# Moving a projection unit forward, eleven scores between the last projection units, and a first attention round cut in two

## The chip, the cores and the metric

The kernel runs on one core of a Trainium2 chip. The metric is the device time of one execution in microseconds (us). The engines of the core are TensorE (PE; its weight loads are shown as PEld), VectorE (DVE), ScalarE (ACT), GpSimd (POOL) and SyncE (SP). Each works through its own queue in the order in which the kernel issues its instructions, and waits for the others by semaphores.

## The reference, cut to what matters

Sequence S = 2048, model width D = 448, 16 heads of width 28, hidden width F = 1792, all float32. The output mixes an attention block and a gated MLP, by a gate for each token:

```python
g = sigmoid((x * gate_w).sum(-1, keepdims=True))
q, k, v = split_heads(x @ wqkv)                 # 16 heads, 28 wide
a = softmax(q @ k.T * 28 ** -0.5) @ v @ wo      # per head, then joined
gate, up = x @ W_gate, x @ W_up
b = (gate * (gate > 0) * up) @ W_down
out = g * a + (1 - g) * b
```

## The kernel before

The projection works in float32r with each operand split into a high and a low part, so one tile of a projection takes 11 matmuls (`TERMS`). Stages, in order:

**Loading.** SyncE loads x in four blocks of 512 tokens (`load_x`, L219) and the projection weights in six slices (`load_w`, L186; `w0` to `w5`, two staging buffers "wr"). ScalarE makes the high parts (`act_high`, L85), VectorE the low parts (`low`, L91); `split_x` and `split_w` issue both.

**Projection units.** There are 44 units. `qk(tb, c)` (L250) makes 128 of the 896 Q and K columns for token block tb: 11 matmuls (L253), a high part by ScalarE and a low part by VectorE into a staging tile `st` (three buffers), and a store by GpSimd to `qk_d` in HBM (L257). `vproj(tb, t)` (L259) makes V for 128 tokens: 11 matmuls (L262) and two ScalarE reads (L265, L266). A unit's PSUM tile comes from `ps_any` (L246), which goes round four banks: two of the scores' ("s"), "x" and "po". Seven `qk` units are written out by hand (L295 to L312); qk(3,0) is the one that first uses the last token block. The others stand in the list `mixed`, where `qk` and `vproj` alternate. At fixed places in it stand `split_w(w5)`, `split_w(w3)`, the loads of head 1's K and Q, and the spills of x.

**Row maxima.** `smax(k)` (L139) makes 128 x 1024 scores of a head (L147, two matmuls into a tile with two buffers) and VectorE reduces them to their maximum (L149). From unit `first` on, `smax` calls are spread evenly behind the units, 2 x `LEAD` = 48 of them. `smax_end` (L154) puts a head's maxima as two extra rows into Q, in float32r halves.

**Scores.** `scores(i, j)` (L168) makes one 128 x 512 tile of the transposed scores of key tile i, with the maxima taken off by the extra rows (L173, PSUM tag "s", two buffers), and ScalarE takes exp of it into `PT[i]` (L175). Four of them (j = 0 to 3) make one key tile. `pv(i)` (L408) then multiplies with V into one accumulator (L413, PSUM tag "po").

**Rounds.** The attention runs in rounds. A round's string says the order on TensorE: "s" a score, "m" a maximum, "x" a matmul of the gate and up projections (`gu_mm`, L380). The scores run one key tile ahead of `pv`. Behind a round's string come the splits of the next gate and up weights (`split_f`, L364; high by ScalarE, low by GpSimd), and then its `pv`. Before the first round four scores, (0,0) to (0,3), have been made: one behind each of the last three units and one after them. The first round is SHORT without its "x": 16 scores and 8 maxima, then four `pv`. The second is SHORT with 11 "x". `small_things` runs at round starts; in the round that starts at key tile 4 it issues `gates` (L348: one ScalarE and three VectorE operations).

**The rest.** The remaining gate and up work, the output projection, the down projection and the mix follow the attention, and are not touched.

Of the kernel before, what the change touches and what calls it, by code (L numbers as in the profile page):

```python
# [27 lines left out]
NB = 4  # L28
# [4 lines left out]
NQ = 2 * D // P  # L33
WARM = 13


LEAD = 24

SHORT = "smsxxsmsxsmsxmsxsmsxxsmsxsmsxxsmsxs"

LONG = "ssmmxsxxsxsmxxsxsmsxxsxxsmmsxxsxxsxsmsxxsmsmsxsxxsxmsmsxxxxsmxssxxmsxsmsxxsmsxmss"
WIDE = "msxxsmsxsxmsxxsxmsxxxxmssmxsxxsxxsmxmssxxxxsxsmsmsxxxxsxsmsxmsxxsxxxsmsmxxxsxsxxxsxmssxmxxss"

LATE = "sxsxxsxsxxsxsxxsxsxxsxsxxsxsxxsxsxsxsx"

ROUNDS = [(SHORT, 0), (SHORT, 1)] + [(LONG, 3)] * 9 + ([(WIDE, 4)] + [(LONG, 3)] * 8) * 2 + [(WIDE, 4)] + [(LATE, 2)] * 6
NP = 9


# [10 lines left out]
def gated_mix_kernel(ctx, tc, x, wq, wo, wgu, wd, out):  # L60
# [8 lines left out]
    def f32(ap):  # L69
        return ap.bitcast(F32)  # L70

    def ps_s(name):
        return psum.tile([P, TB], F32, tag="s", bufs=2, name=name)
# [4 lines left out]
    def ps_o(name):  # L78
        return psum.tile([P, TB], F32, tag="po", bufs=1, name=name)
# [4 lines left out]
    def act_high(dst, src):  # L84
        nc.scalar.activation(dst, src, AF.Copy)  # L85
# [4 lines left out]
    def low(dst, src, high):  # L90
        nc.vector.tensor_tensor(dst, src, f32(high), op=OP.subtract)  # L91
# [22 lines left out]
    def p_slot(k, name, dt=F32):  # L114
        if k in (5, 6):
            return V[:, k - 3].rearrange("p k h d -> p (k h d)").rearrange("p (j t) -> p j t", t=TB)
        return (vp if k < 5 else att).tile([P, 4, TB], dt, name=name, tag=f"P{k}", bufs=1)
# [9 lines left out]
    def load_k(h):  # L127
        for r in range(4):
            nc.sync.dma_start(f32(K[h % 3])[DH * r:DH * (r + 1)], qk_d[r % 2, 2 * DH * h:2 * DH * h + DH, :])

    def load_q(h):
        Q[h] = q_slot(f"Q_{h}").rearrange("p j t -> p (j t)")
        for r in range(4):
            nc.sync.dma_start(f32(Q[h])[DH * r:DH * (r + 1)], qk_d[r // 2, 2 * DH * h + DH:2 * DH * (h + 1), :])
# [4 lines left out]
    def smax(k):  # L139

        h, u, half = maxima[k]
        if u == 0 and half == 0:
            MX[h] = keep.tile([P, 32], F32, name=f"mx_{h}", tag="mx", bufs=2)
        ps = ps_w(f"sm_{k}")
        for c in range(2):
            k0 = (half * 2 + c) * TB
            nc.tensor.matmul(ps[:, c, :], Q[h][:GD, u * P:(u + 1) * P], K[h % 3][:GD, k0:k0 + TB],  # L147
                             start=True, stop=True)
        nc.vector.tensor_reduce(MX[h][:, 2 * u + half:2 * u + half + 1], ps, axis=AX.XY, op=OP.max)  # L149
        if u == NK - 1 and half == 1:  # L150
            M[h] = keep.tile([P, 16], F32, name=f"m_{h}", tag="m", bufs=2)
            nc.vector.tensor_reduce(M[h], MX.pop(h).rearrange("p (a b) -> p a b", b=2), axis=AX.X, op=OP.max)
# [15 lines left out]
    def scores(i, j):  # L168
        h, kt = divmod(i, NK)
        if j == 0:  # L170
            PT[i] = p_slot(i % NP, f"P_{i}")
        ps = ps_s(f"s_{i}_{j}")
        nc.tensor.matmul(ps, K[h % 3][:GD + 2, kt * P:(kt + 1) * P], Q[h][:GD + 2, j * TB:(j + 1) * TB],  # L173
                         start=True, stop=True)
        nc.scalar.activation(PT[i][:, j], ps, AF.Exp, scale=SCALE)  # L175
# [3 lines left out]
    def xf(tb, b):  # L179
        return X[tb][b // 4][:, b % 4]  # L180


    with tc.tile_pool(name="qkv", bufs=1) as pa:
        W = pa.tile([P, 7, 2 * D + VC], F32R, name="W")

        def load_w(c):  # L186
            c0, c1 = c * 2 * GD, (c + 1) * 2 * GD if c < G + 1 else 2 * D + VC
            wr = pa.tile([P, 4, 2 * GD + 2], F32, name=f"wr_{c0}", tag="wr", bufs=2)[:, :, :c1 - c0]
            nc.sync.dma_start(wr, wq[:, :, c0:c1])
            return wr, c0, c1  # L190

        def split_w(wr, c0, c1):

            ways = [(W[:, :, c0:c1], wr)]
            if c0 < 2 * D:
                w, r = (ap.rearrange(f"p c {n} -> p c a j d", a=2, j=4)
                        for ap, n in ((W[:, :, c0:c1], "(j a d)"), (wr, "(a j d)")))
                ways = [(w[:, :, a], r[:, :, a]) for a in range(2)]
            for w, r in ways:
                act_high(w[:, 0:3], r[:, 0:3])  # L200
                low(w[:, 3:6], r[:, 0:3], w[:, 0:3])
            for w, r in ways:
                act_high(w[:, 6], r[:, 3])
                low(w[64:, 6], r[64:, 3], w[64:, 6])
# [36 lines left out]
        def spill_x(tb, r):  # L241
            nc.gpsimd.dma_start(x_d[tb, r], f32(X[tb][r]))

        turn = [3]

        def ps_any(name):  # L246
            turn[0] += 1
            return (ps_s, ps_s, ps_x, ps_o)[turn[0] % 4](name)

        def qk(tb, c, terms=TERMS):  # L250
            ps = ps_any(f"qk_{tb}_{c}")
            for n, (a, b) in enumerate(terms):
                nc.tensor.matmul(ps, W[:, a, c * P:(c + 1) * P], xf(tb, b), start=(n == 0), stop=(n == NT - 1))  # L253
            st = pa.tile([P, 2, TB], F32R, name=f"st_{tb}_{c}", tag="st", bufs=3)
            act_high(st[:, 0], ps)
            low(st[:, 1], ps, st[:, 0])
            nc.gpsimd.dma_start(qk_d[:, c * P:(c + 1) * P, tb * TB:(tb + 1) * TB].rearrange("r d t -> d r t"), f32(st))  # L257
# [21 lines left out]
        ps = ps_o("warm_ps")  # L279
# [29 lines left out]
        w4 = load_w(4)  # L309
        qk(2, 0)  # L310
        w5 = load_w(5)
        qk(3, 0)  # L312
        split_w(*w4)
        w3 = load_w(3)
        load_k(0)
        load_q(0)

        units = [(qk, 2, 1), (qk, 1, 2), (qk, 3, 1), (qk, 2, 2), (qk, 3, 2)]
        units += [(qk, tb, c) for c in range(3, NQ) for tb in range(NB - 1, -1, -1)]
        vs = [(vproj, tb, t) for tb in range(NB - 1, -1, -1) for t in range(4)]  # L320
        mixed = units[:3]
        units = units[3:]
        while units or vs:
            mixed += units[:1] + vs[:1]
            units, vs = units[1:], vs[1:]
        m, first = 0, 8
        spills = {16 + 3 * k: (NB - 1 - k // 2, k % 2) for k in range(6)}
        for n, (f, *a) in enumerate(mixed):
            if n == 1:
                split_w(*w5)  # L330
            if n == 3:
                split_w(*w3)
            if n == 6:
                load_k(1)
                load_q(1)
            if n in spills:
                spill_x(*spills[n])
            f(*a)
            if n >= len(mixed) - 3:
                scores(0, n + 3 - len(mixed))  # L340
            while m < 2 * LEAD and n >= first and m < (n + 1 - first) * 2 * LEAD / (len(mixed) - first):
                smax(m)
                m += 1
                if m == 2 * NK + 3:
                    smax_end(0)
        assert m == 2 * LEAD, m

    def gates():  # L348
        e = const.tile([P, NK], F32, name="e")
# [55 lines left out]
    NI = H * NK  # L405
# [53 lines left out]

    done = sum(n for _, n in ROUNDS) // 2  # L460
    nxt = parts = i0 = 0
# [22 lines left out]
    fetch_f(1)  # L484
    load_k(2)
    load_q(2)
    scores(0, NB - 1)
    wor = None
    for r, (order, nu) in enumerate(ROUNDS):
        ni = order.count("s") // NB  # L490
        late = "m" not in order
        todo = list(range(nxt, nxt + nu))
        nxt += nu
        small_things(i0 // 4)
        if m % (2 * NK) == 0 and i0 <= NI - LEAD:
            smax_end(m // (2 * NK) - 1)
        if late and wor is None:
            wor = load_wo()
        ns = nx = 0
        for o in order:  # L500
            if o == "s":
                i, j = i0 + 1 + ns // NB, ns % NB
                if ns == 4 * NB:
                    small_things(i0 // 4 + 1)
                if i < NI:
                    scores(i, j)
                ns += 1
            elif o == "m":
                smax(m)
                m += 1  # L510
            elif nx < NT * nu:
                i, half = divmod(todo[nx // NT], 2)
                if nx % NT == 0:
                    ps = ps_w(f"gu_{i}_{half}")[:, 0] if late else ps_x(f"gu_{i}_{half}")
                gu_mm(ps, i, half, nx % NT)
                nx += 1
                if nx % NT == 0:
                    (spill_h if half else relu)(i, ps)

        ready = nxt + (ROUNDS[r + 1][1] if r + 1 < len(ROUNDS) else 2)  # L520
        ready += ready % 2
        while parts < ready:
            split_f(parts // 2, pool_low, (parts % 2,))
            parts += 1
            if parts % 2 == 0:
                fetch_f(parts // 2 + 1)
        for i in range(i0, i0 + ni):
            pv(i)
            if i == NI - NK // 2:
                split_wo(wor)  # L530
        i0 += ni
# [154 lines left out]
```

## Time and profile before

| | |
|---|---|
| median of three runs | 1312.54 us (1311.17 to 1313.77) |
| the profiled execution | 1315.21 us, its span 1313.4 us |
| TensorE busy | 1300.0 us (99%) |
| VectorE, ScalarE, GpSimd busy | 799.4 (61%), 770.5 (59%), 360.8 us (27%) |
| granted TensorE clock | 0.999 |
| HBM traffic | 148.87 MB, 113 GB/s over the span |

Busy times are unions of the profile's records, and matmuls overlap each other in them: a busy TensorE may still issue its matmuls with pauses. Pauses are read from the starts of neighbouring matmuls and from the idle times that the timeline prints in square brackets, with what ended them. The span is what lies between the first and the last instruction; the execution's time holds 1.8 us more.

### The profile page before, as it was taken

The numbers are of one execution on the slowest core, as the hardware profiler recorded it, in microseconds if no ns is written. First come the engines' busy times: TensorE is split into PE (matmuls) and PEld (weight loads), VectorE is DVE, ScalarE is ACT, GpSimd is POOL, SyncE is SP. The second block draws the span as 40 slices with busy tenths as digits, with TensorE's granted clock in tenths as the row PEclk, the third lists the DMA queues.
The fourth block names the chain that finished last, engine by engine and source line by source line (L and its number), as shares of the span: only waits on it lengthen the run. The fifth ranks groups of instructions, "written<-read, shape, count | busy, mean of one in ns | idle before, by whom it ended". The sixth has DMA issues, their size and how long they took to land.

```text
span 1313.4 us, 17652 instructions
## 1 busy us (share of the span) xinstructions
PE 1300.0 (99%) x6689; PEld 907.0 (69%) x6689; DVE 799.4 (61%) x811; ACT 770.5 (59%) x1454; POOL 360.8 (27%) x496
## 2 busy tenths in 40 slices
PE   9999999999999999999999999999999999999998
PEld 5888666666666666666666666666666556789997
DVE  6577776676767666766767676767666003663332
ACT  5212686667676676766767667676766785222121
POOL 3212113222222232332313222222322235451020
PEclk9999999999999999999999999999999999999999
DMA  8845515142343624142525324151431225534432
GB/s 294 287 166 219 168 58 106 58 110 67 87 86 91 171 63 89 57 97 66 136 68 158 81 72 97 48 105 41 113 108 55 100 64 180 190 114 147 141 103 74
DMA packets 53533, 148.87 MB, mean 113 GB/s; under 512 B 9992, under 2 KB 17096, under 8 KB 48840
## 3 DMA queue, kind: packets, MB, share of 16 engines
q1 hardware_dynamic: 36520, 98.80, 29.2%
q0 software_dynamic: 16928, 48.93, 10.4%
q8 instruction: 53, 0.87, 0.3%
q14 instruction: 32, 0.26, 0.1%
HBM read 102.06 MB, written 46.02 MB: 113 GB/s over the span
## 4 chain that ended last, share of the span: by engine, by line
PE 93%; DMA 3%; issue 1%; DVE 1%; POOL 1%; ACT 1%; SPq 0%; POOLq 0%; ACTq 0%; DVEq 0%
PE gu L383 21%; PE s L173 19%; PE sm L147 18%; PE po L413 17%; PE acc L606 10%; PE qk L253 3%; PE wo L558 3%; PE v L262 2%; DMA K<-qk_d 1%; DMA qk_d<-st 1%; POOL on L94 1%; DMA wr<-wq 0%; DMA xr<-x 0%; DMA wdr<-wd 0%; PE mt L157 0%
## 5 line engine op out<-in xcount | busy, mean ns | idle before, releaser
L149 DVE TENSOR_REDUCE mx<-sm 128x1 f32<-128x1024 f32 x512 | 610.9, 1220 | 189.5 <-PE sm L147 188.3
L175 ACT ACTIVATE P<-s 128x512 f32<-128x512 f32 x800 | 455.0, 597 | 111.1 <-PE s L173 76.1
L173 PE MATMUL s<-Q,K 114*128 114x512 f32 x1024 | 400.7, 405 | 0.4 <-ACT P L175 0.3
L383 PE MATMUL gu<-X,wg 128*128 128x512 f32 x1232 | 397.0, 396 | 0.0
L147 PE MATMUL sm<-K,Q 112*128 112x512 f32 x1024 | 312.2, 396 | 0.7 <-DMA K<-qk_d 0.5
L173 PEld LDWEIGHTS s<-Q,K 114*128 114x128 f32 x1024 | 190.6, 188 | 108.9 <-ACT P L175 53.1
L383 PEld LDWEIGHTS gu<-X,wg 128*128 128x128 f32 x1232 | 233.5, 190 | 43.9 <-issue 0.8
L147 PEld LDWEIGHTS sm<-K,Q 112*128 112x128 f32 x1024 | 193.0, 190 | 46.6 <-DVE mx L149 2.7
L413 PE MATMUL po<-P,V 128*32 128x512 f32 x1600 | 181.9, 594 | 0.0
L94 POOL TENSOR_TENSOR wg<-wgr,wg 128x384 fp32r<-128x384 f32 x153 | 142.2, 941 | 99.8 <-issue 48.7
L175 ACT ACTIVATE V<-s 128x512 f32<-128x512 f32 x224 | 128.2, 598 | 33.2 <-PE s L173 21.2
L402 POOL DMA_DIRECT2D h_d<-h x56 | 31.7, 566 | 412.2 <-DVE h L396 382.0
L606 PE MATMUL acc<-WD,hh 128*128 128x448 f32 x672 | 140.9, 368 | 0.0
L606 PEld LDWEIGHTS acc<-WD,hh 128*128 128x128 f32 x672 | 126.1, 188 | 12.8
L413 PEld LDWEIGHTS po<-P,V 128*32 128x32 f32 x1600 | 49.1, 110 | 110.5 <-issue 110.5
L85 ACT ACTIVATE hh<-hr 128x512 fp32r<-128x512 f32 x56 | 35.2, 631 | 122.4 <-PE acc L606 118.6
L91 DVE TENSOR_TENSOR hh<-hr,hh 128x512 fp32r<-128x512 f32 x56 | 53.7, 960 | 64.4 <-ACT hh L85 64.4
L396 DVE TENSOR_TENSOR h<-gu,rl 128x512 f32<-128x512 f32 x56 | 38.6, 689 | 87.5 <-PE gu L383 37.3
L253 PE MATMUL qk<-X,W 128*128 128x512 f32 x308 | 76.6, 397 | 2.0 <-ACT X L85 1.8
L253 PEld LDWEIGHTS qk<-X,W 128*128 128x128 f32 x308 | 57.3, 188 | 18.4 <-ACT X L85 2.9
L85 ACT ACTIVATE wg<-wgr 128x384 fp32r<-128x384 f32 x168 | 68.0, 489 | 0.0
L413 PE MATMUL po<-V 128*32 128x512 f32 x448 | 54.1, 594 | 0.0
(58 smaller groups left out, 573.6 us busy)
## 6 DMA issues: line engine op xcount, KB each, us to landing
wgr<-wgu SPq DMA_DIRECT2D x56, 512.0 KB
qk_d<-st POOLq DMA_DIRECT2D x28, 512.0 KB, 3.5
K<-qk_d SPq DMA_DIRECT2D x64, 224.0 KB
Q<-qk_d SPq DMA_DIRECT2D x64, 224.0 KB
h_d<-h POOLq DMA_DIRECT2D x56, 256.0 KB, 2.3
hr<-h_d SPq DMA_DIRECT2D x56, 256.0 KB
x_d<-X POOLq DMA_DIRECT2D x6, 1024.0 KB, 5.0
X<-x_d SPq DMA_DIRECT2D x24, 256.0 KB
```

Source lines behind the costliest of these rows:

```text
L85: nc.scalar.activation(dst, src, AF.Copy)
L91: nc.vector.tensor_tensor(dst, src, f32(high), op=OP.subtract)
L94: nc.gpsimd.tensor_tensor(dst, src, f32(high), op=OP.subtract)
L147: nc.tensor.matmul(ps[:, c, :], Q[h][:GD, u * P:(u + 1) * P], K[h % 3][:GD, k0:k0 + TB], start=True, stop=True)
L149: nc.vector.tensor_reduce(MX[h][:, 2 * u + half:2 * u + half + 1], ps, axis=AX.XY, op=OP.max)
L173: nc.tensor.matmul(ps, K[h % 3][:GD + 2, kt * P:(kt + 1) * P], Q[h][:GD + 2, j * TB:(j + 1) * TB], start=True, stop=True)
L175: nc.scalar.activation(PT[i][:, j], ps, AF.Exp, scale=SCALE)
L253: nc.tensor.matmul(ps, W[:, a, c * P:(c + 1) * P], xf(tb, b), start=(n == 0), stop=(n == NT - 1))
L383: nc.tensor.matmul(ps, WS[i][:, s, a], xf(i // NF, b), start=(n == 0), stop=(n == NT - 1))
L413: nc.tensor.matmul(PO[h][32 * j:32 * j + 32], V[:, h // 4 % 2, kt, h % 4], PT[i][:, j], start=(kt == 0), stop=(kt == NK - 1))
L558: nc.tensor.matmul(ps[:, t % 2, :D], ON[tb][b // 4][:, b % 4, t * P:(t + 1) * P], WO[:, a], start=(n == 0), stop=(n == NT - 1))
L606: nc.tensor.matmul(ACC[tb][t][:, :D], hh[:, a, t * P:(t + 1) * P], WD[:, f, b], start=(f == 0 and n == 0), stop=(f == NF - 1 and n == 2))
```

## The change

Five edits, all of them before the third round:

- qk(2,1) moves from the head of `mixed` to a place ahead of qk(3,0). `mixed` then has 36 units and not 37.
- 50 maxima and not 48 stand behind the units, from the unit with number 9 in `mixed` on, and not 8. Behind the units counted from the end (`EARLY`) stand 2, 3, 3 and 3 scores, eleven in all, ahead of the maxima of the same unit. The single scores behind the last three units and the one after them are gone.
- The four units of the last 128 columns (c = 6) take their PSUM tile from "x" and "po" alone.
- The first round becomes two of two key tiles each. The first has 2 maxima and the one score (2,3) that is left of its eight; the second has 8 scores and 4 maxima.
- The rounds skip the scores that are already made. The number of scores, maxima and all other matmuls is as before. `split_f(0)` stands behind the second of the two rounds.

```diff
+EARLY = (4, 4, 3, 3, 3, 2, 2, 2, 1, 1, 1)
...
-ROUNDS = [(SHORT, 0), (SHORT, 1)] + [(LONG, 3)] * 9 + ([(WIDE, 4)] + [(LONG, 3)] * 8) * 2 + [(WIDE, 4)] + [(LATE, 2)] * 6
+ROUNDS = [("sssssssmms", 0), ("smssmssmsmss", 0), (SHORT, 1)] + [(LONG, 3)] * 9 + ([(WIDE, 4)] + [(LONG, 3)] * 8) * 2 + [(WIDE, 4)] + [(LATE, 2)] * 6
...
-        def ps_any(name):
+        def ps_any(name, late=False):
             turn[0] += 1
+            if late:
+                return (ps_x, ps_o)[turn[0] % 2](name)
             return (ps_s, ps_s, ps_x, ps_o)[turn[0] % 4](name)
...
-            ps = ps_any(f"qk_{tb}_{c}")
+            ps = ps_any(f"qk_{tb}_{c}", c == NQ - 1)
...
         w5 = load_w(5)
+        qk(2, 1)
         qk(3, 0)
...
-        units = [(qk, 2, 1), (qk, 1, 2), (qk, 3, 1), (qk, 2, 2), (qk, 3, 2)]
+        units = [(qk, 1, 2), (qk, 3, 1), (qk, 2, 2), (qk, 3, 2)]
...
-        m, first = 0, 8
+        m, first = 0, 9
...
-            if n >= len(mixed) - 3:
-                scores(0, n + 3 - len(mixed))
-            while m < 2 * LEAD and n >= first and m < (n + 1 - first) * 2 * LEAD / (len(mixed) - first):
+            for k, back in enumerate(EARLY):
+                if back == len(mixed) - n:
+                    scores(*divmod(k, NB))
+            while m < 2 * LEAD + 2 and n >= first and m < (n + 1 - first) * (2 * LEAD + 2) / (len(mixed) - first):
                 smax(m)
...
-    scores(0, NB - 1)
     wor = None
...
-                if i < NI:
+                if len(EARLY) <= i * NB + j < NI * NB:
                     scores(i, j)
```

More of the change, by code (lines that the diff above doesn't have):

```diff
@@ L345, in gated_mix_kernel @@
                     smax_end(0)
-        assert m == 2 * LEAD, m
+        assert m == 2 * LEAD + 2, m
     def gates():
```

## The prediction

> **What bounds the kernel now.** I read the page first, then the waits, then the timelines of TensorE, ScalarE and VectorE over the first 172 us, where all edits lie.
>
> ```profile
> PE 93%; DMA 3%; issue 1%; DVE 1%; POOL 1%; ACT 1%; SPq 0%; POOLq 0%; ACTq 0%; DVEq 0%
> ```
>
> The chain that ended last is TensorE's. So a change counts by what it does to TensorE's pauses; its matmuls stay the same in number. I found pauses by the starts of neighbouring matmuls (steady: 0.232 us in `qk`, 0.205 in `vproj`, 0.234 in maxima and scores). TensorE's timeline of the projection stage:
>
> ```profile
> 24.99 13.30 PE L253 MATMUL qk<-X,W 128*128 128x512 f32 x55 [1.33 <-ACT X L85]
> 38.24 2.88 PE L262 MATMUL v<-W,X 128*128 128x450 f32 x11
> 51.24 1.17 PE L147 MATMUL sm<-K,Q 112*128 112x512 f32 x4 [0.55 <-DMA K<-qk_d]
> 64.13 1.40 PE L147 MATMUL sm<-K,Q 112*128 112x512 f32 x4
> ```
>
> Line one is qk(3,0) waiting for the last tokens. Line two: the first `vproj` takes 2.88 us, its sisters 2.42 (it waits for `split_w(w3)`). Line three: the first maxima wait for K. Line four: two maxima take 1.40 us where others take 1.09; the second waits for a maximum buffer. Then TensorE, ScalarE and VectorE where the scores begin:
>
> ```profile
> 142.47 0.40 PE L173 MATMUL s<-Q,K 114*128 114x512 f32 x1
> 142.71 0.62 PE L147 MATMUL sm<-K,Q 112*128 112x512 f32 x2
> 143.16 0.39 PE L173 MATMUL s<-Q,K 114*128 114x512 f32 x1
> 143.81 0.50 PE L173 MATMUL s<-Q,K 114*128 114x512 f32 x1 [0.25 <-ACT P L175]
> 144.14 0.64 PE L147 MATMUL sm<-K,Q 112*128 112x512 f32 x2
> ...
> 142.67 0.60 ACT L85 ACTIVATE st<-qk 128x512 fp32r<-128x512 f32 x1 [2.62 <-PE qk L253]
> 143.16 4.88 ACT L175 ACTIVATE P<-s 128x512 f32<-128x512 f32 x8
> ...
> 143.90 10.30 DVE L149 TENSOR_REDUCE mx<-sm 128x1 f32<-128x1024 f32 x9
> ```
>
> From 143.16 to 153.59 run 17 scores and 8 maxima, 17 x 0.235 + 16 x 0.234 = 7.7 us of matmuls in 10.4 us. With two score buffers, every second score waits for an exp.
>
> **Removed.** (a) qk(2,1), all of whose inputs are ready by 21.3 us (end of X[2]'s low part), fills the pause before qk(3,0). From 23.26 to 24.99 is 1.50 us over a matmul's time; three more starts inside qk(3,0), late by 0.1 to 0.18 for the same data, come to 0.39. -1.9.
> (b) The scores' stretch: 2.7 us over its matmuls, 0.1 of it the entry to `pv`. -2.6.
> (c) The wait for K before the first maxima, 0.55 shown, 0.79 with the slow restart. The first maxima move back by two `qk` units (5.1 us), while K's load waits for qk(3,0)'s store, now the eighth and not the seventh (issued 34.04, not 31.91). K and Q of head 0 landed by 51.1; 1.7 to 3.7 later is 52.8 to 54.8, and TensorE comes there at about 55. -0.8; bounds -0.8 and +1.
>
> **Given back early.** (d) ScalarE's reads of `qk` into `st` wait for stores (three buffers):
>
> ```profile
> 32.42 0.60 ACT L85 ACTIVATE st<-qk 128x512 fp32r<-128x512 f32 x1 [0.60 <-DMA qk_d<-st]
> 37.33 1.23 ACT L85 ACTIVATE W<-wr 128x336 fp32r<-128x336 f32 x4 [0.94 <-DMA wr<-wq]
> ```
>
> `split_w(w4)` stands behind qk(3,0)'s read. That was read seven (30.29), and becomes read eight (32.42). So the staging slot that w4 frees, and w3's load on SyncE behind it, move from 32.88 to about 35.0, and its landing from 37.3 to 39.4. The first `vproj` got its second matmul 1.56 us after that landing (38.83), so now at 41.0. TensorE, without (a)'s pause, comes there at 38.8. Wait: 2.1 us, was 0.6. +1.5. Bounds: 0 if other work had covered the load (nothing does: the next units stand behind), +3 if w3 landed as slowly as the slowest stores do. The Trainium skill, "DMA: Bandwidth & Descriptors", section "Queues, rings and completion order", has each DMA engine go round-robin between queues by packets; by it w3, now beside stores eight and nine, would get half of the 300 GB/s or so that this stage moves and take 3.0 us for its 448 KB, an estimate 0.6 above what it took, and the sum below would be +4.1. I keep the row of w3's own load.
>
> (e) Maxima come 50 in 27 units (1.85 each) and not 48 in 29. VectorE needs 1.13 us for each, plus 0.6 for `st`'s low part behind a `qk` unit. Where both units of a pair bring two maxima, the last one waits: four times in the trace (64.81, 84.15, 103.50, 123.00), 0.31 each. In the built order of the changed kernel I count eight such pairs. +1.2; bounds 0 and +2.
>
> **Given back at the end of the units.** (f) The scores now stand three in a row behind a unit (two in the first), with two buffers, and ahead of that unit's maxima. Take t as the start of the unit's last matmul. ScalarE first reads the unit (142.24 to 142.67: t+0.43), starts the first exp 0.49 later (143.16), ends it at 143.75, and the third score starts at 143.81: t+1.57. Unhindered it would start at t+0.70. Wait 0.87, and 0.1 for the matmul that restarts (143.81 to 144.14 is 0.33, not 0.235). All of this is the row above, only with a maximum between the scores; in the new order nothing is between. Behind `vproj` it is the same with 0.49 for its two reads: 1.0. In the first unit (vproj(0,2)) the second score needs the buffer which that `vproj` itself used, 0.7. Four units: 0.7 + 1.0 + 1.0 + 1.0 = 3.7. Bounds: 2.6, if the first unit and the restarts cost nothing, and 4.5; a gain is excluded, since no matmul is saved.
>
> What stands behind the stopped score are the maxima, ready all the while: at 144.14 in the row their buffer had been free since 142.5. The Trainium skill, "TensorE: Matmul & The Clock Gate", section "Step-by-step: what each phase is for", says that matmuls stay in program order and that only weight loads are pulled ahead. The row agrees; if maxima could pass, two of them (0.93 us) would fill each pause and the sum would be near zero.
>
> (g) One maximum of the last unit, then two of the first round, stand in a row. The third needs the first's buffer: reduce 1.22 us, matmul end and hand-overs 0.5, against 0.7 unhindered: 1.1 with the restart.
> (h) The second round of two has eight scores and four maxima. ScalarE has run dry during the two `pv` before it, so the first pair is free; three pairs cost 0.26 each, as pairs do in the old stretch (144.61 to 145.33). 0.8. Bounds 0.3 and 1.3.
> (i) `split_f(0)` and `gates` come closer behind that round, and VectorE enters SHORT with up to 1.5 us of maxima in hand: 0.3, bounds 0 and 1.1. The weights of `gu` were done 0.6 us before their use (157.58, 158.20). Their load waits for the last `st` store, which moves with the units. I cost it at nothing, hidden by the `pv` of that round (1.8 us); without that cover, up to 1.
> (j) Two `pv` runs for one: entry and leaving take 0.1 each. +0.2.
> SyncE's head-1 and head-2 loads and GpSimd's spills move with the units and are used over 5 us after they land.
>
> **Sum.** Early: -1.9 - 0.8 + 1.5 + 1.2 = 0.0. Late: -2.6 + 3.7 + 1.1 + 0.8 + 0.3 + 0.2 = +3.5. In the rounds from there on TensorE pauses by 0.03 us here and there, apart from the entries to and from `pv`, so the sum is carried to the end. The profiled execution took 1315.21 us (span 1313.4, 1.8 around it), 2.7 above the median of 1312.54. Against its own time: 1318.7; on the median: **1316.0**.
>
> **Rivals.**
> *Cheap middle, within 0.2%.* w3 lands earlier ((d) +0.5), fewer pairs wait ((e) +0.6), (i) nothing: +1.6, 1314.1. For it: (d) and (e) rest on loads and counts, not on rows of the same order. Against: reads seven and eight are 2.1 us apart in the trace.
> *Faster.* Exps of eleven scores run beside 10 us of unit matmuls, where ScalarE is 27% busy (130 to 140 us). Place: the third score of a unit; it decides when its wait is under 0.2 us, as if ScalarE emptied the first score before the third is due. Then (f) is 0.6, (g) half, (h) 0.3: late -2.6 + 0.6 + 0.6 + 0.3 + 0.2 = -0.9; early, with (d) at 0, -1.5, and with (e) near its lower bound -2.5: -2.4 to -3.4, so 1309.6. Against it: 1.57 against 0.70 in the same rows.
> *More slowly still.* K or w3 lands 2 us later than worked out, as stores here took between 3.6 and 11.8 us to land; or `gu`'s weights lose their cover as well: +5 to 7, 1318.5.
> *The filling fails.* If qk(2,1) itself waited, (a) would be lost: +5.4, counted with the last.
>
> **How the numbers follow.** 0.2% is 2.6 us, about what a measurement of this kernel can tell. Forecast 0.60 (own range +2.4 to +4.6), cheap middle 0.17, faster 0.10, more slowly 0.13. Slower by over 0.2%: nine tenths of the forecast's case, and the last: 0.67. Within: cheap middle, 0.06 of the forecast's and some of the faster: 0.24. Faster: 0.09. The range leaves out most of the faster case and the end of the slow one: 1311.0 to 1318.8.
>
> **What would show it.** Right: no pause at qk(3,0); the first `vproj` about 4.4 us; no wait at the first maxima; about eight maxima waits of 0.3; in the last four units a score that waits for ScalarE some 0.9 each; a maximum ahead of the first `pv` waiting 1.0. Wrong: third scores without a wait, or a first `vproj` of 2.9 us.

## The result, and the profile after

The changed kernel takes 1319.00 us (median of six runs, 1317.55 to 1320.76) where the kernel before takes 1312.05 beside it: a ratio of 1.0052, 95% interval 1.0039 to 1.0065. It is slower, as forecast, but by 6.95 us and not by 3.5, and 0.2 us past the end of the range. Two further series of the same program, told below, gave 1.0036 (1.0024 to 1.0048) and 1.0043 (1.0029 to 1.0058).

The page of the changed kernel still has a chain made of TensorE:

```profile
PE 93%; DMA 2%; DVE 1%; ACT 1%; issue 1%; POOL 1%; SPq 0%; POOLq 0%; ACTq 0%; DVEq 0%
```

TensorE's timeline of the projection stage (start, length, engine, line, operation; in brackets the idle time and what ended it; lines have moved on by two to six: L257 is `qk`, L266 `vproj`, L149 a maximum, L175 a score, L419 `pv`):

```profile
21.79 4.54 PE L257 MATMUL qk<-X,W 128*128 128x512 f32 x19
...
42.75 4.17 PE L266 MATMUL v<-W,X 128*128 128x450 f32 x11 [3.27 <-ACT W L87]
46.75 2.69 PE L257 MATMUL qk<-X,W 128*128 128x512 f32 x11
...
58.84 1.09 PE L149 MATMUL sm<-K,Q 112*128 112x512 f32 x4
...
62.01 1.40 PE L149 MATMUL sm<-K,Q 112*128 112x512 f32 x4
...
68.97 1.40 PE L149 MATMUL sm<-K,Q 112*128 112x512 f32 x4
```

The pause ahead of qk(3,0) is gone: the first row runs through it with no bracket. The first maxima (58.84) wait for nothing. Instead the first `vproj` waits for `split_w(w3)`, and then takes 4.17 us for its eleven matmuls where the later ones take 2.42. The 1.40 rows are the pairs of maxima whose second waits; there are eight, as counted. The same timeline at the end of the units:

```profile
136.43 0.39 PE L175 MATMUL s<-Q,K 114*128 114x512 f32 x1
137.29 0.50 PE L175 MATMUL s<-Q,K 114*128 114x512 f32 x1 [0.47 <-ACT zt L270]
...
142.44 0.50 PE L175 MATMUL s<-Q,K 114*128 114x512 f32 x1 [0.71 <-ACT P L177]
...
147.33 0.50 PE L175 MATMUL s<-Q,K 114*128 114x512 f32 x1 [0.72 <-ACT P L177]
...
152.51 0.50 PE L175 MATMUL s<-Q,K 114*128 114x512 f32 x1 [0.71 <-ACT P L177]
152.85 1.09 PE L149 MATMUL sm<-K,Q 112*128 112x512 f32 x4
154.79 0.77 PE L149 MATMUL sm<-K,Q 112*128 112x512 f32 x2 [0.86 <-DVE mx L151]
155.37 0.62 PE L175 MATMUL s<-Q,K 114*128 114x512 f32 x1
155.92 3.31 PE L419 MATMUL po<-P,V 128*32 128x512 f32 x16
```

The five waits that the forecast worked out stand here one by one. What it did not have is the last row: 16 matmuls of `pv` in 3.31 us. The windows show why. Columns are the stretch, its length, then busy time and number of instructions of TensorE, its weight loads, VectorE, ScalarE and GpSimd, then the granted TensorE clock, the DMA share and GB/s:

```profile
39.30:42.71 3.41, 0.18 (x1) 0.00 (x0) 1.04 (x2) 1.47 (x4) 1.45 (x2) 1.00 1.02 349
42.72:46.13 3.41, 3.38 (x8) 2.78 (x9) 1.72 (x5) 0.94 (x3) 0.61 (x1) 0.50 0.97 341
46.13:49.54 3.41, 3.41 (x17) 2.88 (x16) 0.00 (x0) 0.67 (x3) 0.12 (x1) 1.00 0.94 314
151.94:155.35 3.41, 1.99 (x7) 1.35 (x8) 2.53 (x3) 1.60 (x4) 0.71 (x1) 1.00 0.33 127
155.36:158.77 3.41, 3.41 (x18) 0.60 (x16) 1.64 (x2) 0.60 (x1) 0.00 (x0) 0.50 0.47 163
158.77:162.18 3.41, 3.41 (x15) 1.84 (x11) 2.01 (x2) 2.27 (x5) 0.00 (x0) 1.00 1.03 296
```

Behind a window with 0.18 us of matmuls, and behind one with 1.99, the clock is 0.50 for exactly 3.41 us, and then 1.00 again. One such stretch lies on the first `vproj`, the other on the first `pv`. They begin at 42.72 and 155.36, 33 lengths of 3.413 us apart: within one execution I lay the windows on that grid, and where no half clock falls early I take it from a later switch of the same trace. The Trainium skill, "TensorE: Matmul & The Clock Gate", section "What's actually happening", gives the clock two levels, full and half, and has an idle window of some 3.4 us followed by half rate. The levels and the length agree with these rows; the 1.99 us of matmuls in the second window do not make it idle, so the measured condition is wider than the sentence.

### The profile page after: what moved, and what is told of

It reads as the page before. It is cut to its first block, busy times and chain, and to the rows that moved or that the text cites. A ratio compares the mean times of both kernels' runs of the same rounds, so it can differ in the third digit from the quotient of the medians.

```text
span 1319.0 us, 17655 instructions
## 1 busy us (share of the span) xinstructions
PE 1303.3 (99%) x6689; PEld 907.4 (69%) x6689; DVE 798.0 (60%) x811; ACT 769.8 (58%) x1454; POOL 359.9 (27%) x496
## 4 chain that ended last, share of the span: by engine, by line
PE 93%; DMA 2%; DVE 1%; ACT 1%; issue 1%; POOL 1%; SPq 0%; POOLq 0%; ACTq 0%; DVEq 0%
PE gu L389 21%; PE s L175 19%; PE sm L149 18%; PE po L419 17%; PE acc L611 10%; PE qk L257 3%; PE wo L563 2%; PE v L266 2%; DMA xr<-x 1%; DMA qk_d<-st 1%; DVE mx L151 1%; POOL on L96 1%; DMA wr<-wq 0%; DMA hr<-h_d 0%; ACT st L87 0%
## 5 line engine op out<-in xcount | busy, mean ns | idle before, releaser
L175 PE MATMUL s<-Q,K 114*128 114x512 f32 x1024 | 400.4, 405 | 2.7 <-ACT P L177 2.1
L149 PE MATMUL sm<-K,Q 112*128 112x512 f32 x1024 | 312.0, 396 | 1.2 <-DVE mx L151 0.9
L175 PEld LDWEIGHTS s<-Q,K 114*128 114x128 f32 x1024 | 190.4, 188 | 112.5 <-ACT P L177 54.5
L149 PEld LDWEIGHTS sm<-K,Q 112*128 112x128 f32 x1024 | 192.3, 190 | 48.3 <-DVE mx L151 5.6
L419 PE MATMUL po<-P,V 128*32 128x512 f32 x1600 | 183.4, 598 | 0.0
L419 PEld LDWEIGHTS po<-P,V 128*32 128x32 f32 x1600 | 49.2, 110 | 111.4 <-issue 111.4
L257 PE MATMUL qk<-X,W 128*128 128x512 f32 x308 | 76.2, 397 | 0.5 <-ACT X L87 0.2
L257 PEld LDWEIGHTS qk<-X,W 128*128 128x128 f32 x308 | 57.6, 188 | 16.4 <-DVE X L93 1.7
L93 DVE TENSOR_TENSOR mh<-mr,mh 16x128 fp32r<-16x128 f32 x16 | 4.5, 279 | 82.6 <-ACT mh L163 82.6
```

The source lines that it names most:

```text
L419: nc.tensor.matmul(PO[h][32 * j:32 * j + 32], V[:, h // 4 % 2, kt, h % 4], PT[i][:, j], start=(kt == 0), stop=(kt == NK - 1))
```

## The yardstick

What follows the first rounds varies from execution to execution by more than the question: from the first matmul of the fifth `pv` tile to the end it took 1142.7 to 1146.9 us in the profiled executions of all kernels here (1145.95 in the kernel before, 1142.90 in the changed one). So I compare profiles at the start of that matmul, ahead of which every kernel has done the same work, and timings by their ratios. Of the kernel before only one execution has a profile here, so how far its 167.48 spreads is not known. Between them stands the excess: the time between starts of neighbouring matmuls less their undisturbed pace (0.232 us for `qk`, 0.205 `vproj`, 0.234 maxima, 0.235 scores), summed over a stretch. The rows follow each other in time; a wait counts in the row in which it ends, and a half-clock stretch where it falls.

| Excess, us | before | changed | again (e5) | third (e12) | late edits alone (e2) | w4 ahead (e4) | e8 | e9 |
|---|---|---|---|---|---|---|---|---|
| the first qk | 1.47 | 2.04 | 1.69 | 1.74 | 1.71 | 1.40 | 1.78 | 1.58 |
| to the first vproj | 2.36 | 0.56 | 0.35 | 0.38 | 2.32 | 0.35 | 0.37 | 0.37 |
| around the first vproj | 0.57 | 5.18 | 2.76 | 4.53 | 0.19 | 2.46 | 0.51 | 0.44 |
| to the first maxima | 0.67 | -0.06 | -0.06 | -0.04 | -0.04 | -0.06 | -0.06 | -0.06 |
| to the first score | 1.33 | 2.43 | 2.48 | 2.47 | 2.20 | 2.42 | 2.41 | 0.97 |
| first score to last qk | -0.04 | 2.71 | 2.71 | 2.71 | 2.43 | 2.68 | 0.34 | 0.34 |
| last qk to first pv | 2.69 | 2.41 | 2.42 | 2.55 | 2.17 | 2.18 | 1.27 | 1.26 |
| first pv to first gu | 0.24 | 2.72 | 2.71 | 2.58 | 1.34 | 1.32 | 1.34 | 1.34 |
| to the fifth pv tile | 0.16 | 0.21 | 0.21 | 0.19 | 0.22 | 0.22 | 0.23 | 0.20 |
| fifth pv tile at | 167.48 | 176.09 | 173.30 | 175.10 | 170.36 | 170.97 | 166.01 | 164.38 |

## The experiments

My theory after the result: the forecast's terms hold, but the wait for w3 is larger, and the waits bring half-clock stretches that the forecast did not price. The rivals: another term is wrong (e1, e2 and e7 tell which half and which wait), or the first execution was an odd one (e5, e12).

**The halves: e1, the early edit alone, and e2, the late edits alone.**

```diff
# e1: the kernel before, with
+        qk(2, 1)
         qk(3, 0)
...
-        units = [(qk, 2, 1), (qk, 1, 2), (qk, 3, 1), (qk, 2, 2), (qk, 3, 2)]
+        units = [(qk, 1, 2), (qk, 3, 1), (qk, 2, 2), (qk, 3, 2)]
...
-        m, first = 0, 8
+        m, first = 0, 9
# e2: the changed kernel with these lines as they were before, qk(2, 1) back at the head of mixed
```

> The early edit alone: qk(2,1) stands ahead of qk(3,0) and the maxima start at unit 9 of the list; scores, rounds and the 48 maxima are those of before. Theory A (the first vproj's wait for w3, and a halved TensorE clock behind that long wait, make over half of the loss): the pause at qk(3,0) is gone (-1.9 us), the first vproj takes 2 to 5 us longer, its matmuls 0.37 us each if the wait is over 3.4 us; +1 to +4 us against the kernel before. Theory B (the loss lies in the scores between the last units): -1 to +0.5 us against before.

> The late edits alone: eleven scores behind the last four units, 50 maxima, two rounds of two key tiles; the units stand in the order of before and the maxima start at unit 8. Theory A: +3.5 to +4.5 us against before by the waits of the third scores, the maxima in a row and the two pv runs, and one more us or two where a window of the clock with long waits is followed by one at half the clock. Theory B: +6 us or more. A third one (the exps hide beside the units): below 0.

Measured: e1 1314.68 us, ratio 1.002 (1.0009 to 1.003), the fifth `pv` tile at 171.08; e2 1316.82, ratio 1.0033 (1.002 to 1.0046), at 170.36. Each half costs. In time, 0.2% and 0.33% make 0.53%, beside 0.52, 0.36 and 0.43% in the three series of the changed kernel. At the fifth `pv` tile, 3.6 and 2.9 us make 6.5, between the 5.8 and 8.6 of the changed kernel's executions. So the early edit, which I had put at 0.0, loses 1.8 us by the medians and 3.6 at that tile; e1's profile is of the slowest of its ten runs (1318.97 us). Its timeline (L262 is `vproj` there):

```profile
42.87 3.91 PE L262 MATMUL v<-W,X 128*128 128x450 f32 x11 [3.33 <-ACT W L85]
```

The late edits alone have no such wait (38.14, 2.59 us, no bracket), and their excess from the first score on is 6.16 us against 3.05: +3.1, where I had worked out +3.5.

**The same program again: e5 and e12.**

> The changed kernel once more, for its spread and as the yardstick of the three others. If the halved clock windows depend on where the clock's 3.4 us windows fall (theory A), the first vproj waits for w3 by 2 to 4.5 us in any execution, but the number of halved windows is 0, 1 or 2, and its times spread by 3 us or more. If the wait alone made the loss, the times stay within 1 us.

> The changed kernel unaltered, a third time, on the chip of e11. My theory: the waits of the last units are as before (0.47, 0.71, 0.72, 0.71, 0.86 in the brackets of the timeline) in every execution; the wait of the first vproj lies between 2 and 3.3 us, by when the stores of the first units land; a half-clock stretch of 3.41 us at the first pv in most executions, since the last pauses are the same in each. Ratio to the kernel before 1.0035 to 1.0055. The rival, that the first execution was an odd one: a ratio below 1.003 and no half clock in the first 170 us.

Measured: e5 1318.66 us, ratio 1.0036 (1.0024 to 1.0048); e12 1319.11, ratio 1.0043 (1.0029 to 1.0058). The first `vproj` of e5, then of e12:

```profile
41.18 2.90 PE L266 MATMUL v<-W,X 128*128 128x450 f32 x11 [2.11 <-ACT W L87]
```

```profile
41.83 4.06 PE L266 MATMUL v<-W,X 128*128 128x450 f32 x11 [2.73 <-ACT W L87]
```

The waits of the scores are the same to 0.01 us in all three executions; the wait for w3 is 3.27, 2.11 and 2.73. In e5 no half-clock stretch follows it, and the `vproj` takes 2.90 us: the stretch costs 1.2 to 1.3. The five runs of e5 lie within 2.75 us, between the 3 or more of the one theory and the 1 of the other. All three executions have a half-clock stretch at the first `pv`. In e5:

```profile
149.15:152.56 3.41, 1.98 (x7) 1.35 (x8) 2.52 (x3) 1.61 (x4) 0.71 (x1) 1.00 0.32 125
152.56:155.97 3.41, 3.41 (x18) 0.59 (x16) 1.66 (x2) 0.60 (x1) 0.00 (x0) 0.50 0.39 141
```

The single runs carry a mark as well, though not a place: of e5's two stretches one lies at 1149.25 us, far behind the edits. One stretch lowers an execution's mean clock by 3.41 x 0.5 / 1318 = 0.0013. Of the 17 runs of the changed program, 10 have a mean clock of 0.998 or less; of the 77 runs of the kernel before that stood beside the experiments, 14 do. In the first series the four runs at 0.997 took 1318.8 to 1320.8 us, the other two (0.998 and 0.999) 1317.8 and 1317.5.

**e3, TensorE kept awake during the wait for w3, and e4, `split_w(w4)` ahead of qk(3,0).**

```diff
# e3
             ps = ps_any(f"v_{tb}_{t}")
+            if (tb, t) == (NB - 1, 0):
+                for _ in range(12):
+                    nc.tensor.matmul(ps, warm[:, :P], warm, start=True, stop=True)
# e4
+        split_w(*w4)
         qk(3, 0)
-        split_w(*w4)
```

> The changed kernel with 12 matmuls of a zero bf16 tile (0.216 us each, 2.6 us) ahead of the first vproj's own, in its PSUM tile, so that TensorE works through most of the wait for w3; the first real matmul overwrites them. Theory A (an idle TensorE is what halves the clock): the wait for w3 ends when it did, the granted clock stays 1.0 around 43 us, and the first vproj's matmuls take 0.2 us each, not 0.37: 1.0 to 1.2 us less than the changed kernel. Rival (the vproj's matmuls are slowed by transfers, not by the clock): they still take 0.37 us, and the time is the same or higher.

> The changed kernel with split_w(w4) issued ahead of qk(3,0), between the seventh and the eighth read of a projection tile. Theory A (w3's load waits on SyncE for w4's split, and that stands behind the eighth read, which waits for the fifth store): w3's load is issued 1.5 to 2.5 us earlier, the first vproj waits 1 us or less, the clock stays whole there: 3 to 5 us less than the changed kernel. Rival (w3's load is late because stores eight and nine run beside it): the load is issued earlier but lands no more than 0.5 us earlier, and the time falls by under 1 us.

Measured: e3 1317.78 us, ratio 1.0036 (1.0022 to 1.005); e4 1317.66, ratio 1.004 (1.0024 to 1.0055). In e3's profile w3's load was issued at 34.4 us and no half clock came, but w3 was early there by itself, so e3 does not tell the theories apart. e4 is a miss: I had expected 3 to 5 us less than the changed kernel. w3's load did go out early, at 33.00, but its split on ScalarE now stood behind the read of qk(2,2), which waited for a store until 38.95, and the first `vproj` began at 40.34. In this chain of reads, moving one split only changes which store is waited for.

Both show the price of the late half-clock stretch, since neither has one there. e4's window and its first `pv`:

```profile
149.46:152.87 3.41, 2.55 (x16) 1.23 (x18) 2.86 (x3) 1.17 (x2) 0.71 (x1) 1.00 0.40 154
152.87:156.28 3.41, 3.41 (x20) 1.48 (x12) 1.86 (x3) 1.62 (x4) 0.00 (x0) 1.00 0.66 221
```

```profile
152.19 1.92 PE L419 MATMUL po<-P,V 128*32 128x512 f32 x16
```

The same 16 matmuls, behind the same waits (0.71 and 0.86), take 1.92 us instead of 3.31. From the first score on, e4's excess is 6.40 and the changed kernel's 8.05: the stretch costs 1.6. What differs is where the windows of 3.41 us begin: in e4 the one that holds the last wait also holds 0.7 us of `pv`. The seven executions with these waits in place divide by that. Where the window before had 1.84 to 1.99 us of matmuls, the half clock came (the three of the changed kernel and e6); where it had 2.24 to 2.56, it did not (e2, e3, e4).

**e6, all splits where the kernel before has them between the reads; e7, scores and maxima in turn; e8, both.**

```diff
# e6 and e8: w4 ahead of qk(3, 0) as in e4, and
-            if n == 1:
+            if n == 0:
                 split_w(*w5)
-            if n == 3:
+            if n == 2:
                 split_w(*w3)
# e7 and e8: behind a unit, a score, then a maximum, then the next score
-            for k, back in enumerate(EARLY):
-                if back == len(mixed) - n:
-                    scores(*divmod(k, NB))
...
+            line = [k for k, back in enumerate(EARLY) if back == len(mixed) - n]
...
+                if line:
+                    scores(*divmod(line.pop(0), NB))
```

> The changed kernel with the three weight splits at the places among the reads that they had before: split_w(w4) between the seventh and eighth read, split_w(w5) at n == 0, split_w(w3) at n == 2. Theory A: w3's load is issued near 33 us, its split no longer stands behind the read that waits for the eighth store, the first vproj waits under 1 us and no halved window follows: 4 to 6 us less than the changed kernel, +1 to +3 us against before by the late part. Rival (w3's load is slow because it shares the DMA engines with two stores): the first vproj still waits 2 us or more, and the time falls by under 2.5 us.

> The changed kernel with the scores and the maxima of the last four units in turn (score, maximum, score, maximum, score), not all scores first. Theory (the third score waits for an exp with ready maxima behind it): the four waits of 0.7 to 1.0 us become 0.1 to 0.5, the three maxima in a row wait 0.6 and not 1.1: 3 to 4 us less than the changed kernel. Rival (ScalarE's whole load in these units sets the pace): the waits move to the maxima or the next unit, and the time falls by under 1 us.

> Both mends at once. If both theories hold the gains add: the pause at qk(3,0) and the wait for K are gone as meant, the first vproj waits under 1 us, the last units wait 1 us in all: 1 to 3 us below the kernel before. If they share a cause (a single late transfer or a full ScalarE), the sum of the two gains is missed by 2 us or more and the time stays above before.

Measured: e6 1318.02 us, ratio 1.0026 (1.0016 to 1.0037); e7 1315.87, ratio 1.0021 (1.0012 to 1.0029); e8 1312.72, ratio 0.9995 (0.9986 to 1.0003). In e6 the excess around the first `vproj` is 0.45 us, so with its splits in place the early edit waits no longer than the kernel before (0.51 and 0.44 in e8 and e9; e10, below, waits longer). The time is a miss: 0.6 us less than e5 by the medians, where I had expected 4 to 6 less, though the fifth `pv` tile comes 2.2 us earlier, at 171.14 (a half-clock stretch stands at its first `pv` as well, 150.03 to 153.44). e7 takes 2.8 us less than e5, where 3 to 4 was expected. In it the waits of the third scores are gone, which shows (f) to be the order alone: with a maximum between them, the third score no longer stops TensorE.

```profile
135.42 0.40 PE L175 MATMUL s<-Q,K 114*128 114x512 f32 x1
135.66 0.63 PE L149 MATMUL sm<-K,Q 112*128 112x512 f32 x2
136.12 0.40 PE L175 MATMUL s<-Q,K 114*128 114x512 f32 x1
136.36 0.63 PE L149 MATMUL sm<-K,Q 112*128 112x512 f32 x2
136.82 0.44 PE L175 MATMUL s<-Q,K 114*128 114x512 f32 x1
```

These are rows of e8, one unit's scores and maxima without a bracket; the excess from the first score to the last `qk` is 0.34 in e7 and e8, where it was 2.71. No half-clock stretch falls at the first `pv` in either. With both causes taken away the fifth `pv` tile comes at 166.01 in e8, 1.5 us ahead of the one profile of the kernel before. In time the loss is gone; a gain is not shown, since the interval holds 1.

**e9, e8 with the first of two maxima inside the unit, and e10, the early edit alone with its splits in place.**

```diff
# e9: e8, and where two maxima fall behind one unit
-            f(*a)
+            inside = None
+            if first < n < len(mixed) - 4 and m + 1 < (n + 1 - first) * (2 * LEAD + 2) / (len(mixed) - first):
+                inside = one_max
+            f(*a, mid=inside)
# in qk and vproj, behind the matmul with n == 5
+                if mid and n == 5:
+                    mid()
```

> This is e8 (the splits between the reads as before, a key tile's maxima and a unit in turn), and where two maxima fall behind one unit, the first of them is issued after the unit's sixth matmul. My theory: the eight waits of 0.31 us at the second maximum of a pair, as in the changed kernel's trace, come from VectorE having a low part and two maxima to do behind one unit, so with the first maximum a half unit earlier they vanish: 2.0 to 2.5 us less than e8, the first matmul of the fifth pv tile at 163.5 to 164.2 us (e8: 166.0), a ratio to the kernel before of 0.997 to 0.998. The rival: the maximum in the middle of a unit finds its PSUM buffer not yet free, or pushes the low part and the reads behind it, and the waits only move: less than 0.5 us gained, ratio 0.999 to 1.000.

> The kernel before with the early edit alone (one unit of query tile 2 in front of that of the last tokens, nine units between reads and 48 maxima), but the splits of w4, w5 and w3 left between the reads where the kernel before has them. My theory: the pause at qk(3,0) (1.9 us) and the wait for K (0.8) stay removed, the wait of the first vproj for w3 is at most 0.6 as in e6 and e8, and the pairs of maxima cost some 0.6: 1.0 to 2.5 us less than before, ratio 0.998 to 0.9992, the fifth pv tile at 165.0 to 166.5 us. The rival: with the old scores' stretch as before, the wait for w3 or K comes back, or a half-clock stretch falls in the waits of the maxima: no gain, ratio 1.000 to 1.002.

Measured: e9 1311.19 us, ratio 0.999 (0.9981 to 0.9998), the fifth `pv` tile at 164.38; e10 1312.68, ratio 1.0001 (0.9992 to 1.001), at 167.02. In e9 the maxima between 60 and 129 us wait for VectorE no more. Who waits for whom at the tile "sm", of the changed kernel first, then of e9:

```profile
who waited for it (us, times):
  PEld sm L149: 3.8, 8
```

```profile
who waited for it (us, times):
  DVE mx L151: 6.3, 10
```

It is now VectorE that waits for maxima. The excess of that stretch falls from 2.41 to 0.97; 0.9 of what is left is one wait, at 56.46 us. So the pairs cost what was counted, though the gain in time, 0.1% against the kernel before, is smaller than the 0.2 to 0.3% expected. e9 is the fastest of the kernels here, and ahead of the kernel before by little: its interval ends at 0.9998. e10 went as its rival has it: the pause at qk(3,0) stays away, but where `vproj` was to wait 0.6 at most it waits longer, the first maxima wait for K again, and no gain is left:

```profile
40.05 2.91 PE L262 MATMUL v<-W,X 128*128 128x450 f32 x11 [0.94 <-ACT W L85]
...
55.41 0.94 PE L147 MATMUL sm<-K,Q 112*128 112x512 f32 x3 [0.35 <-DMA K<-qk_d]
```

In that execution the seventh read of the units started at 31.96 us, by its store's landing, and not at 30.5 as in e6; all behind it moved by as much.

**e11, the last two pauses filled.**

```diff
+    def fill(count):
+        ps = ps_x("fill")
+        for _ in range(count):
+            nc.tensor.matmul(ps, warm[:, :P], warm, start=True, stop=True)
...
+                    if k == 10:
+                        fill(3)
                     scores(*divmod(k, NB))
...
+                if r == 0 and m == 2 * LEAD + 3:
+                    fill(4)
                 smax(m)
```

> The changed kernel with seven extra bf16 matmuls of zeros (0.215 us each, into a bank that is free then): three ahead of the third score of the last unit, four ahead of the maximum that waits for VectorE in front of the first pv. They lie in pauses of 0.72 and 0.86 us and move nothing else. My theory: the half clock at the first pv comes from how little TensorE streams in the 3.41 us before; with the two pauses filled no half-clock stretch begins there, the first 16 pv matmuls take 1.9 us and not 3.3, and where e12 shows a half-clock stretch at the first pv, this run is 1.4 to 1.6 us earlier at the fifth pv tile (about 171.5 where w3 costs what it did in the second execution of the changed kernel). In time 1 to 2 us less than e12. The rival: the half clock has nothing to do with the pauses (power, or chance): it comes here too, the first pv takes 3.3 us, and the time is e12's or up to 0.3 us more.

Measured: 1319.27 us, ratio 1.0048 (1.0033 to 1.0063), the fifth `pv` tile at 171.53. Timeline and windows:

```profile
148.67 0.82 PE L173 MATMUL fill<-warm 128*128 128x512 bf16 x3
149.54 0.50 PE L180 MATMUL s<-Q,K 114*128 114x512 f32 x1
149.88 1.09 PE L149 MATMUL sm<-K,Q 112*128 112x512 f32 x4
150.81 1.04 PE L173 MATMUL fill<-warm 128*128 128x512 bf16 x4
151.83 0.73 PE L149 MATMUL sm<-K,Q 112*128 112x512 f32 x2
152.40 0.40 PE L180 MATMUL s<-Q,K 114*128 114x512 f32 x1
152.73 1.93 PE L426 MATMUL po<-P,V 128*32 128x512 f32 x16
```

```profile
149.78:153.19 3.41, 3.41 (x17) 1.58 (x20) 2.64 (x3) 1.15 (x3) 0.71 (x1) 1.00 0.40 154
153.19:156.61 3.42, 3.42 (x24) 1.55 (x16) 1.86 (x2) 1.62 (x4) 0.00 (x0) 1.00 0.62 170
```

The score and the maximum start as late after the unit as before; only TensorE is not idle, and the first `pv` takes 1.93 us at full clock, with the fifth `pv` tile where I had put it (its wait for w3, 1.67 us, was also 0.4 shorter than e5's). That does not settle whether the pauses are the cause. The first `pv` starts 2.95 us into its window here; in e4 and e3 it starts 2.73 and 2.16 into it, and these kept the full clock without any filling. The changed kernel's own matmuls, laid on e11's windows, come to 2.70 and 2.56 us, which are e4's figures (2.70 and 2.55). So e11 would most likely have kept its clock unfilled, and what speaks for the pauses is the comparison of windows under e4. The timings show no gain either: 1319.27 against e12's 1319.11, with intervals that overlap, where 1 to 2 us less was expected. Four of e11's six runs have a mean clock of 0.997, and only one, at 0.999, has a profile; where the others' stretches lay is not to be seen, the wait for w3 being one place left.

## Why the prediction was wrong in size

Right, term by term, from the table and the timelines:

- (a) forecast -1.9: the excess up to the first `vproj` went from 2.36 to 0.56, 0.35 and 0.38.
- (c) -0.8: from 0.67 to about zero in all three executions. That the edit did it is not shown: e2, in the order of before, has no wait for K either (its maxima start at 50.13), and e10, with the early edit, has one again (0.35 in the bracket).
- (e) eight pairs, +1.2: +1.1.
- (f) 3.7: starts late by 0.62, 0.87, 0.88 and 0.87, and 0.1 for each restart, 3.6. (g) 1.1: 0.86 in the bracket, 1.1 with hand-over and restart.
- (h), (i), (j) together 1.3: the excess from the first `pv` to the first `gu`, without a half-clock stretch (e2, e4), went from 0.24 to 1.3, so 1.1. `gu`'s weights kept their cover.
- The late sum +3.5: 6.40 less 3.05 makes 3.4 in e4, 3.1 in e2.

The step that failed first is (d), put at +1.5 with bounds 0 and +3. The queue was as described, but numbers in it were off. The load of w3 was to be issued at 35.0; it was at 36.53 (e5: 35.16, e12: 35.70), since read seven waited for its store until 32.73 (31.36 in e5) where the trace of before has 30.29. From issue to the start of its split it was to take 4.4 us; SyncE's and ScalarE's rows of the changed kernel:

```profile
36.53 0.54 SPq L191 DMA_DIRECT2D wr<-wq  x1
```

```profile
41.84 1.23 ACT L87 ACTIVATE W<-wr 128x336 fp32r<-128x336 f32 x4 [1.51 <-DMA wr<-wq]
```

That is 5.3 us, 5.1 in e5 and 5.2 in e12. In e6, e8 and e10, where the load stands ahead of one store more, it took 4.6 to 4.7. The sentence of the Trainium skill, "DMA: Bandwidth & Descriptors", section "Queues, rings and completion order", that I had set aside would have added 0.6 to w3's load beside the stores. The load took 0.7 to 0.9 longer, so in size the sentence was nearer than the row that I kept. The trace agrees with it only in part: w3's packets took 2.64 us from first to last, and 2.14 in the kernel before, but the stores moved 264 KB in that time and not as much as w3's 448; the first packet also came 0.35 us later behind the issue. Without half clock, (d) cost 3.3, 2.2 and 2.8 us: 0.7 to 1.8 more than forecast.

One number was off the other way: the forecast has read eight 2.1 us behind read seven, as in the trace of before, and in the three executions it stands 1.2 behind (33.94, 32.56 and 33.10). That gives back 0.9, about what the load took longer. What is left is read seven. In the six executions that have this order and no filling at the first `vproj`, its start and the wait in the bracket are 30.96 and 1.67 (e11), 31.36 and 2.11 (e5), 31.88 and 2.73 (e12), 31.94 and 2.52 (e7), 32.73 and 3.27 (the first execution), 32.78 and 3.33 (e1). At the 30.29 that the forecast took over from the kernel before, the same line would give a wait of about 1.1, an estimate. So the late landing of that store made (d) too small; why it lands when it does stays open.

Under (d) lies something that the forecast and the runs left alone. w3 is columns 672 to 895 of `W`, and `vproj` reads columns 896 and on, which come with w4 and w5. So the first `vproj` uses no value of w3, and still it is held until that split has written: its first two matmuls start at 42.75 and 43.34, 0.05 us behind ScalarE's second row of the split and 0.06 behind VectorE's. The splits of w4 and w5 had ended by 38.42, and TensorE was there at 39.48. The first unit that reads w3 is qk(3,5), 17 units behind that `vproj`. No run put `split_w(w3)` behind the first `vproj`, so what that would save is not measured.

The second is a step that was not there at all: every pause was priced by its own length, at a clock that the page of before gives as 0.999. The signs that the forecast named for the first `vproj` missed this too: the row of the changed kernel reads 4.17 us, near the 4.4 of "right", but by half clock, with the wait ahead of it in the bracket; that is luck. e5's row reads 2.90, the sign of "wrong", behind a wait of 2.11. The half-clock stretches cost 1.3 + 1.6 us in the first execution, 1.6 in e5 and 1.2 + 1.6 in e12.

The sums for the fifth `pv` tile: forecast 3.5, plus (d)'s excess 1.8, 0.7, 1.3, plus half clock 2.9, 1.6, 2.8, plus 0.6, 0.2, 0.3 in the first `qk`: 8.8, 6.0 and 7.9 us. Measured: 8.6, 5.8 and 7.6. The medians say 6.95, 4.99 and 6.15.

Of the rivals, "more slowly still" came nearest in time (1318.5), and one half of its mechanism happened: w3 was split 41.8 us after the start instead of 39.4. Its other half, the weights of `gu`, did not. "Cheap middle" fell with (d), which grew, and with (e), which had its eight pairs; "faster" fell with (f), which was as priced. What stays open is how much of the median the half clock makes: no run takes it away with the waits left as they are.

## What to carry to other kernels

A unit pulled forward into a pause also pulls its buffer traffic forward: where reads, splits and stores share one queue, count the splits' places between the reads and move them with it (e6 and e8 against the changed kernel), or the pause comes back at the next load. Ask of such a wait, too, whether the instruction that waits reads what it waits for; here it did not. When several short waits of TensorE are put close together, price them twice: once by their length, and once by the slower matmuls behind them, with the granted clock in windows of 3.41 us. Work that depends on a slow reader goes in turn with work that does not (e7, e8): 2.4 us here, at the scores, for the same instructions in another order.

## What the runs showed of the hardware

- The clock falls to 0.50 for 3.413 us, or for two such lengths in a row (e7, 41.18 to 48.01), and the cut is sharp: the `vproj` matmuls within it start 0.37 us apart and not 0.205.
- How little work brings it is not settled. In the first 170 us, windows with 0.18, 0.95, 1.43, 1.47, 1.84, 1.85, 1.98 and 1.99 us of matmuls were followed by half clock; windows with 1.91, 2.03, 2.24, 2.55 and 2.56 were not. Near 1145 us, in the output projection, a window of 1.68 was followed by full clock in the kernel before and by half clock in e1 and e5.
- Whether bf16 matmuls of zeros in the pauses keep the clock up is not shown: e3 and e11 had full clock with them, but by their windows or their short wait they may have had it without.
- The landing of the same store differs by over 2 us between executions. Up to read seven the twelve executions with the early edit issue the same work, and its start, which waits for that store, lies between 30.40 (e4) and 32.78 us (e1). So a wait behind such a chain is a range, not a number.
